# An attention-then-FFN kernel on one core: the order of its steps, its PSUM banks and the choice of masked half rows written anew

## The chip, the cores and the metric

One core of a Trainium2 chip runs the whole program. The metric is device time in microseconds (us), the median of the executions shown. The engines are named as in the profile: PE (TensorE, matmuls; PEld are its weight loads), DVE (VectorE), ACT (ScalarE), POOL (GpSimd) and SP (SyncE, which issues most DMAs). They run side by side, each in its own program order, and wait for each other by semaphores.

## What is computed

Eight batches of eight heads, 576 positions, head size 64; the attention keeps only scores close to the row's maximum; its result, 4608 tokens of 512 values, goes through a feed-forward layer that takes the largest of three products.

```python
scores = scale * np.matmul(q, k.transpose(0, 1, 3, 2))
thresh = np.max(scores, axis=-1, keepdims=True) - tau
scores = np.where(scores >= thresh, scores, -1000000000.0)
scores = scores - np.max(scores, axis=-1, keepdims=True)
attn = np.exp(scores)
attn = attn / (np.sum(attn, axis=-1, keepdims=True) + 1e-09)
x = np.matmul(attn, v)        # then heads side by side: (4608, 512)
h = np.maximum(np.maximum(x @ w1, x @ w2), x @ w3)
out = h @ w_out
```

## The kernel before

The work is cut into small steps, and the order in which the program issues them is written out by hand, as a string of letters (`ORDER`, lines 40 to 74). A loop at the end of the kernel (lines 789 to 796) takes one letter after the other and issues its step. Since every engine takes its instructions in program order, the string sets the order on each engine; between engines only data and buffers matter. A capital letter is a step of PE that opens a PSUM tile, and the digit behind it is the place of that tile: PSUM is used as four slots of two banks (`bank`, line 182).

Four heads of one batch make a quad, 16 quads in all. A quad has nine chunks of 128 rows by two halves (two heads side by side), and each chunk has two half rows r = 0 and 1, 288 in all. Through a half row go, in this order:

- S: scores, float32, on PE, one PSUM slot (`scores`, line 324).
- m: DVE copies the scores to an SBUF tile z, with the sign turned, and takes the row maximum (`maximum`, line 364). There are 9 z tiles, and from the 73rd half row on two more that lent themselves from the weight staging.
- s: DVE makes a threshold out of the maximum (`threshold`, line 375), for code 0 only.
- e: ACT's first pass (`exponents`, line 379); n: ACT's second pass, an exponential with its sum; k: in its place, for masked half rows, a pass of DVE that compares, multiplies and sums (`numerators`, line 388).
- r, once for a chunk: DVE takes reciprocals of the sums. p, once for a half row: POOL scales z into the bfloat16 tile P (`normalized`, line 400; 6 tiles P).
- t, once for a chunk: SP issues a DMA that transposes P into `ptq` (`turned`, line 409).

`MASKED` (lines 24 to 29) gives each half row a code. 0: first pass of ACT from z with the threshold of s, then n. 1: masked, so ACT's first pass is the exponential, from z, and k takes the second pass to DVE. 2: like 0, but ACT reads the scores from PSUM, no s is needed, and the PSUM slot is held until ACT has read it. 3: like 1, but from PSUM.

```python
    def masked(g, idx, r):
        return by_mask[2 * number[g, idx] + r] in "13"
    def direct(c, r):
        return by_mask[2 * number[c["g"], c["idx"]] + r] in "23"
```

The other letters: l loads of q, k and v, g loads of weights, o and i stores of the output (all on SP, with t); z casts of weights, y casts of v and q swaps of the halves of q (POOL, two swaps on DVE); T transposes of q and k on PE (line 293), with a (ACT) and c (DVE) for their copies out of PSUM; O the product of attention and v (line 415), with x (ACT) and w (DVE) for its copies into x of the batch; F and B the two halves of a piece of the FFN (lines 457 and 479), N a last ninth of the output product; h (ACT), v (DVE), u and j (ACT), f (DVE) empty their PSUM. A batch has 18 hidden-layer pieces and its output pieces; they can begin when the four O of the batch are done. Batch 7 is split into two parts, so that its FFN begins earlier.

Of the kernel before, what the change touches and what calls it, by code (L numbers as in the profile page):

```python
# [45 lines left out]
nyrrsmyBepT1svS0hpcT2nS3zmaS1erpgsF2mntpsBmnS3yvF1etssT0myeBprS2cnpS3mnS0ympelF2epF3lmBnzslssvS0htBrqmeS2vpn  # L46
S1gF0sepmF3teqBmF2erssvpBtnBkphF0eS1vtS3znmF2nrBmqteS1rpvBnS3pmlnF0pmgeS1qsBsrhmS3pevS2npS1mF0npsO3ermpesmO2
zewepgsskBxtT3nF1vS2nklBarS0mlphS3mtepF2sS1rmnyBmetF3pvT0eBpcnS2tzT1nvS0asmzS3temS2qeS1meF0trkpmS3lenpBmnlys
reklpF1umerpskS3upBeoketmS0uS2umpS3tesmS1qeT0myO2nqlrsnlprcO3etqsmepwS0xptS1mnF3psnmS2BlerskpS1thF0meF3pmeBF
2ktnBveBsrS1nvpS0hmyF3emF2npBrssT0eprtvBaF1kS3nqvBeF0myhyS2kyleF3mBelBvnpS2snsS0vptemS1pnF3rmpT2tnBmpeF0scS1  # L50
# [5 lines left out]
eBptsF2mhpS1eS3pmteS0qmBeO1spmnkteF3rvnpT0BsskapS2xvS0erS1qmtnS3pmnF2mqlespmeS1rtkBepresmT3puS1cuS0ptmnS3pS2
meyS1lrekpF0tnsmempO3lekteskO2nrsmpeBkpxrnwS1uptS3muS2pnmF0yoeS1mF3lesymBtnS2srkpS1hmBeF0spveF2ertBmpT3nrsvS
1paBlmpnS0tS3qhmF1epsmS2leBymF3tevF0nBknlS1rsvpS2esmqnBF3srmhpS1epS0tmeF2pssBrempBtesvS0ynF1mT3lnpBvF0lhsrcS
2tnT1mBnF3valS2nrBsqmeF0pvS1epS2meBptsmS3eqF1hmT2peBcS3tnskT2O0arkplnmO2lerpvewptS3xkpS1nF2meF0sstreBsmpS3nv
# [1 line left out]
ymeF3pwxskteS0keS1BrrnkopmF2pmS0BqeuurtsmF1phS3srnpS2meT0ptBmeS3ykpaN2esvempF0tS1jkpF3ermBeS2ptvnS1pmBnS0rls
hsmpS2elF3mqntS1mpF0nsrBskpeF2lsmBetBpveF1yhvS3lnkS2lesF0mytnBmBerqsS3veF2lpvnF1pBsmT0htBceF3rT2vnpBsaS0pvnF
1qmtS2nBsrnmT0pS3hrcpF2esS1mpteS0rmpS3emBpntF1svqnS0ssBmpeoT2vO3lamtneF1wS0nrlBpmeS3qsrS2hsmS0pnmF1eptS3smeB
pmF2ntS0veS3rsmnpS1BnpO0veytrempS2empS3xsmS1tekF0nsknlT2rmpBelmlpnscS3quS1umyS2eorT0kpeO3tmeyO1ewlepsmF3etka
rknS2qklT0nBmxespcS2eryF0mpF1uskpuBtnS2BhmqF3nsvS0peS2srmtpF1eBmpeF0srvnBptS2hyS3pmeF1lmeBlBevtF3nkT2S0arrvp
BnS2mphS1smpF0ntS3smnpBmeF1lsT2esvlF3nrBrcptBnvpS2eS0qmlhS1tsnprsmT3F2epmS0aptBemF3yevS1oS0nqmBnpsrS2mnF1ptv
S0epmBeS3mthS2skeF0F1snmlBeklO3ersvpnrmByepF0swT2eqtBvnqF3ssrcS1hpiBmpT0S2vaptS1snmS0pnT3mqF2tecT1BarmS3pnS1
vqeS0mF2pesrmnptmS3npT1seS0qctBeymqermpS1eS3mpuF0nmtuskS1eS2klnS3smBesrsepO1upmemO2txrkpukeO3wnkpS0xS2emF3et
rmS1pnBssspmF2hS0rtepS3mnBpmF1etS0veF3mnN2rnpBpjF0evtF2esBkBkhF1nsvS3eBmBevO3hrkS2pwnS1mnF3prmS2eptsF0mnBpsS
1sevyS2terBmpeF3svS1iyepBmoS0yhmtF2ekF3nBsmS1ersBvpnF0pmeF2BvteS1hBmF3rsS0vpeF1rknpBBmnO2vhptO0xrpnS3pwS2trm  # L70
# [759 lines left out]
```

## Time and profile before

| | us |
|---|---|
| median of three runs | 446.92 |
| lowest and highest | 445.95, 449.74 |
| span of the profiled execution | 444.8 |

The profiled execution's time is listed only among the three runs and not by name; its span, from the first to the last instruction, is 1.1 us below the lowest of them. Other groups of the profile that matter for reading the code:

| group | count | busy us |
|---|---|---|
| scores on PE (two groups, qs and qt) | 1280 | 182.6 and 182.4 |
| hidden-layer products on PE | 2160 | 170.8 |
| ACT first pass from z, with threshold (z tiles) | 143 | 106.2 |
| ACT second pass with sum (z tiles) | 174 | 117.6 |
| DVE maximum (z tiles) | 250 | 183.7 |
| DVE masked second pass (z tiles) | 76 | 62.2 |
| POOL scaling into P (z tiles) | 250 | 200.6 |

Busy times of groups overlap on one engine and don't add up to its busy time. In the rows of the profile, `z` and `stage` are tiles of half rows, `sc` the scores in PSUM, `ph` hidden-layer products, `po` output products, `o` the product with v, `tp` transposes. All instructions of the kernel carry line L93, that of a helper that keeps the order, so groups are told apart by tile.

### The profile page before, as it was taken

The page shows a single profiled execution, that of the slowest core. Times are in us where ns is not written, and L with a number is a line of the kernel's source. Part 1 is how long each engine was busy: PE and PEld are TensorE (multiplying, and loading weights), DVE is VectorE, ACT ScalarE, POOL GpSimd, SP SyncE. Part 2 cuts the span into 40 slices and gives each one's busy share as a digit, 9 for nine tenths or more (in the row PEclk, how much of TensorE's full clock was granted, in tenths as well). Part 3 has the DMA queues.
Part 4 walks back from the last instruction along what each step waited for, and adds up shares of the span by engine and source line. Part 5 has one row for each costly group of instructions (what it writes and reads, how often), then busy time and mean ns, then how long its engine had stood idle before and what let it go on. Part 6 is the DMA issues. An engine that isn't in the chain of part 4 may idle for free.

```text
span 444.8 us, 14254 instructions
## 1 busy us (share of the span) xinstructions
PE 422.4 (95%) x5188; PEld 320.2 (72%) x5190; DVE 392.8 (88%) x1228; ACT 403.0 (91%) x836; POOL 311.9 (70%) x420
## 2 busy tenths in 40 slices
PE   7767789999999999999999999999999999999996
PEld 6334347787788767787788777788688886787873
DVE  3887999999999999999999999998999998899642
ACT  3999999999999999999999999899999999987632
POOL 2799989997878687696785877676676685457400
PEclk8998999999999999999999999999999999999999
DMA  7999999999999999699899999989999977487633
GB/s 188 275 293 199 291 169 269 235 243 262 229 180 194 212 222 292 125 256 167 143 234 189 230 198 203 209 168 210 208 206 194 244 151 105 83 179 136 145 116 108
DMA packets 213959, 88.50 MB, mean 199 GB/s; under 512 B 189184, under 2 KB 202240, under 8 KB 213888
## 3 DMA queue, kind: packets, MB, share of 16 engines
q1 hardware_dynamic: 213360, 86.96, 95.9%
q8 instruction: 41, 0.67, 0.6%
q10 hardware_dynamic: 528, 0.62, 0.5%
q14 instruction: 30, 0.25, 0.2%
HBM read 35.65 MB, written 9.44 MB: 101 GB/s over the span
## 4 chain that ended last, share of the span: by engine, by line
PE 86%; ACT 5%; DVE 4%; issue 2%; DMA 1%; SPq 0%; DVEq 0%; ACTq 0%
PE ph L93 32%; PE sc L93 32%; PE po L93 10%; PE o L93 9%; ACT z L93 5%; PE tp L93 3%; DVE z L93 3%; DMA qm<-in_q_dram 1%; ACT qt L93 1%; SPq L93 0%; DVE xt L93 0%; DVE hm L93 0%; DVE stage L93 0%; DVE rs L93 0%; ACT ob L93 0%
## 5 line engine op out<-in xcount | busy, mean ns | idle before, releaser
L93 POOL TENSOR_SCALAR P<-z,rs 128x576 bf16<-128x576 f32 x250 | 200.6, 814 | 63.3 <-DVE rs L93 28.1
L93 DVE TENSOR_SCALAR_CACHE_REDUCE z<-sc 128x576 f32<-128x576 f32 x250 | 183.7, 750 | 14.8 <-PE sc L93 10.1
L93 PE MATMUL sc<-kt,qs 64*128 64x256 f32 (+2 forms) x640 | 182.6, 423 | 5.7 <-DVE z L93 2.3
L93 PE MATMUL sc<-kt,qt 64*128 64x320 f32 (+2 forms) x640 | 182.4, 433 | 5.2 <-ACT z L93 3.3
L93 PE MATMUL ph<-xt,w 64*128 64x288 bf16 (+2 forms) x2160 | 170.8, 283 | 0.1
L93 PEld LDWEIGHTS <-w 64*128 64x128 bf16 (+1 forms) x2160 | 130.1, 94 | 28.6 <-issue 4.3
L93 ACT ACTIVATE z<-z 128x576 f32<-128x576 f32 x174 | 117.6, 679 | 0.1
L93 PEld LDWEIGHTS sc<-kt,qs 64*128 64x128 f32 (+1 forms) x640 | 92.4, 180 | 25.7 <-DVE z L93 5.7
L93 ACT ACTIVATE z<-z,th 128x576 f32<-128x576 f32 x143 | 106.2, 769 | 5.0 <-DVE th L93 4.2
L93 PEld LDWEIGHTS sc<-kt,qt 64*128 64x128 f32 (+1 forms) x640 | 91.9, 179 | 19.7 <-ACT z L93 5.9
L93 DVE SCALAR_TENSOR_TENSOR z<-z 128x576 f32<-128x576 f32 x76 | 62.2, 830 | 0.5 <-ACT z L93 0.5
L93 PE MATMUL po<-wo,hT 64*128 64x512 bf16 (+3 forms) x454 | 53.5, 354 | 0.3
L93 POOL COPY qs<-qt 64x640 f32<-64x640 f32 (+3 forms) x66 | 43.0, 652 | 10.8 <-ACT qt L93 7.2
L93 ACT ACTIVATE z<-z,nm 128x576 f32<-128x576 f32 x68 | 50.6, 767 | 0.0
L93 DVE TENSOR_TENSOR hm<-ph,hm 128x576 bf16<-128x576 f32 (+2 forms) x54 | 37.0, 686 | 9.2 <-PE ph L93 8.9
L93 ACT ACTIVATE hm<-ph 128x576 bf16<-128x576 f32 (+2 forms) x54 | 31.8, 589 | 13.4 <-PE ph L93 12.8
L93 POOL TENSOR_SCALAR P<-stage,rs 128x576 bf16<-128x576 f32 x38 | 30.4, 804 | 19.3 <-ACT z L93 5.4
L93 PEld LDWEIGHTS <-hT 64*128 64x128 bf16 (+2 forms) x456 | 30.0, 95 | 16.5 <-issue 2.3
L93 DVE TENSOR_TENSOR hT<-ph,hm 128x576 bf16<-128x576 f32 (+2 forms) x54 | 37.0, 686 | 4.0 <-PE ph L93 2.3
L93 PE MATMUL o<-ptq,vb 128*64 128x64 bf16 (+2 forms) x544 | 39.0, 281 | 0.0
L93 ACT ACTIVATION_READ_ACCUMULATOR z<-z 128x1 f32 x174 | 34.3, 197 | 0.0
L93 PEld LDWEIGHTS <-vb 128*64 128x64 bf16 x544 | 23.3, 111 | 12.8 <-issue 4.9
(45 smaller groups left out, 431.6 us busy)
## 6 DMA issues: line engine op xcount, KB each, us to landing
vm<-in_v_dram SPq DMA_DIRECT2D x32, 256.0 KB, 4.8
qm<-in_q_dram SPq DMA_DIRECT2D x15, 512.0 KB, 5.0
km<-in_k_dram SPq DMA_DIRECT2D x15, 512.0 KB, 5.3
out_dram<-ob SPq DMA_DIRECT2D x14, 512.0 KB, 4.0
stage<-in_moe_w_dram SPq DMA_DIRECT2D x9, 512.0 KB, 5.2
ptq<-P SPq DMA_TRANSPOSE x144, 4.0
vr<-in_v_dram SPq DMA_DIRECT2D x16, 128.0 KB, 3.4
stage<-in_moe_w_out_dram SPq DMA_DIRECT2D x3, 512.0 KB, 4.9
```

The lines of the kernel that those rows point to most:

```text
L93: ins = fn(*a, **kw)
```

## The change

Only the two strings are changed: `MASKED` (109 of its 288 codes) and `ORDER` (3465 letters before, 3477 after; the slots' digits not counted). No function is touched. Letters of each kind are the same in number, but for n (202 to 198), k (86 to 90) and s (169 to 181). The codes go from 169, 78, 33 and 8 of kinds 0, 1, 2 and 3 to 181, 86, 17 and 4. Below are all codes; of the order its first five lines (the start, up to the first F), then the lines with the 10th to 12th O and with the 19th and 20th O, and its end. All the other lines change in the same way.

```diff
 MASKED = """
-232222322322222222021032222202332122123122200200111000000000100000000011
-000010111020011000101000000001100001001000010011111100000000100100000000
-110010030111000100010000000001010100001110001011010100110000000000000000
-100101101011000000120000001010000000110000011100000001110001000010011111021
+112200200001110011002221222020211232320300202100110000000000100000100011
+000011101001000100110000000000110000011000011010101000100001000010001000
+110010010011100101000000001000110100000001101101001100010100001000001000
+100001010110110000000000000010100000011010111011001010000010100010103021
 ORDER = """
-llllllglllT0laclT1laclzllqqS0qqS1meS2mS3lmlT0enlkS1ylmlT2eamelrnpS3leqlmnyS1qcapS0emtnrcS3pmnT2qmepgrelS1qya
-gS0pmelT2mqnS3tcpemqS2nlkT1eytaS0rmnT1kpermS3yS2enczrmS1qT0enmepnqtS3nprmaymgpeS0lptS2mppT0mtpS1enencnqsS3re
-rmtpS0mS1penmS3lqnsS2mtperpekzllmT0tmpenkT1pgS3eearnS0petmnqrS2meqlnpS3lmnplsS2cetpremS1pS0nmplermtzeS3mnS2p
-mtnpmS3rkpS1leektS0emnrpmemptS1eekS2pO3mktS0rennmpermT2pnS1wptemS3prkyO0tmeakS2pgS1enxlnrmS0lpesS2mezT3mS1np
-mgntspcS2eqrseT3mtpeS0srmapS1mnT2ptS3mnqO0ceqmeO1prswnptnkS3pxS0meF1meS2zBresmT0qghF3klpF2nkBtaS1sveS0pemF3B
+llllllgllT2lcaqqlT3S0alcqqmS1lzS3elmS2gmS0elmelkeT1lkaT2nlqS3maqlnsmS0qgeqrrscS3ylecmnS2lpmS1nlpmepsserS2mzS
+0lesmS1pnmS2ynlpmS3nprmT1eS0ymgpaT2lspsnT3mT1ezcS0esrqS2akeptcelmpT1eknqmerqkS3etqalrekpS2gnmnS0psmteysS3emp
+nrS1kpT2emntT0yrmepncytS3pnrS2mpetmpaS1repS3mtepknpS2ntmS0elzmelmS1pnlsS3rmpnT2rspectmepS2epgS0mnqmS2eqS0tme
+qS1emlqO3nrklpnweptrnmS2zeO3mepknpS1xrS0metpmnT2pS3rketpasS1meS0ptrmeT2psnkS1tpemnzrmtS0nscS3pemtepS2knT0qS1
+atmnrlS0rspmempeS2tmyngO1meplssrepS2lwnS3gpmeS0lkqO2elmelmyT1xpS3srceS0pmF2npS1mnBqtmnF3qsrhkT0pBakS1esS2veF
...
-O1ypersmqO2etkpemO0lewqxlknpS3tS1keF2momS3lexF0ktT1enkBercpnsBpumN1ertkphkF3jS0rursS1empBnmF2ptS0vpS1smeF3yt
+mS2nS0mtS3ermpO1esspmnO2yemnkyO0tesrkpewF3epkxS2reBymxpkelqF2ulS0npBlmnN1srshkptuT0nS2cqF3jmyS0erS1semBptnmF
...
-pBnmS1tS2hmT3eF0rmpnF1cBpnBrevptT3S2apvS0qmtS3S1enmqF2esrsqmiepmleS0soykeS1plBnmemtS3ukS0uT1snrlO2cpekynO1me
+rmpesmepO0knuO1wekuT3ekF0xrrclpeS2slpnBmpktpF2ursS3uS1pemBopmS0nlyS3hmF1emS2teS0srsmpT3nBmeN2vatkeqS1lkjF0on
...
-2tvF3vF1hF2voF3vF1ohF2vF3vF1hF2vO3vO1wF2xuuF1oF0hiF3vF1vF0hF3vF1vF0hF3vF1vF0hF3vF1vF0hF3vF1vF0huF3vF1ovF3uoF
-0uoN1fjdi
+F3voF2hF1vF3vF0htF2vF3vF0hF2vF1vF0hF2vF3vF1hF2vO3vO2wF0xF2uF1hF0voF3vF1hiF0vF2vF1hF3vF0vF2hF1vF0vF3hF2vF0vF1
+hF3vF2vF0uF1ouN3ofjdi
 """
```

More of the change, by code (lines that the diff above doesn't have):

```diff
@@ L24 @@
 MASKED = """
-232222322322222222021032222202332122123122200200111000000000100000000011
-000010111020011000101000000001100001001000010011111100000000100100000000
-110010030111000100010000000001010100001110001011010100110000000000000000
-100101101011000000120000001010000000110011100000001110001000010011111021
+112200200001110011002221222020211232320300202100110000000000100000100011
+000011101001000100110000000000110000011000011010101000100001000010001000
+110010010011100101000000001000110100000001101101001100010100001000001000
+100001010110110000000000000010100000011010111011001010000010100010103021
 """
@@ L46 @@
[L46 to L50, printed above, removed]
@@ L51 @@
-htBrnmpF3erT2rpvlBasS1pstvnS2pmeF0pS3emtBqnmT2S1hcqS3empF2eS0rsqmtS1epsmBeF3pmnF0stsvBeBknF2klhF1BvelS0nrvpB
-emT3pS2arvS0ptnS3mpnO1smtesrkpeF2swnlrpmeT0S1qtescS3epBmnpmnT0trskS3paS1umS0ulqmeS3lmyS1nopS2smelS0rmeS3psmn
-O1ypersmqO2etkpemO0lewqxlknpS3tS1keF2momS3lexF0ktT1enkBercpnsBpumN1ertkphkF3jS0rursS1empBnmF2ptS0vpS1smeF3yt
-BsnsmBpnvS0pT1hmF2atT3srepS0cF1eprBsmeqF3vnByBynvplS2nsS0plmhS1mteS2mF0nF3mteS1rrspBnmS2pelvBlepF1smT0leqBvl
-aS2rkhF3oqnsS0mtS1epmBeqsF2ssmtS0epvBeyF1mnF3vpBesrS0ktphBermS1npT2svO0nytmpncT3eS1wF2nrmS0aBrsmnqF3vnT1pS0c
@@ L56 @@
[L56 to L59, printed above, removed]
-pBnmS1tS2hmT3eF0rmpnF1cBpnBrevptT3S2apvS0qmtS3S1enmqF2esrsqmiepmleS0soykeS1plBnmemtS3ukS0uT1snrlO2cpekynO1me
@@ L61 @@
[L61 to L70, printed above, removed]
@@ L71 @@
-npS0mnF3pmteF1pBeBvtS0rS2vpS3empF1ktkF0kBereskpemBkperumO2uptO3xpN1wtenkO2jrF3pxF1hpF2nvF3tvF1rhF2pvF3pvF1hF
-2tvF3vF1hF2voF3vF1ohF2vF3vF1hF2vO3vO1wF2xuuF1oF0hiF3vF1vF0hF3vF1vF0hF3vF1vF0hF3vF1vF0hF3vF1vF0huF3vF1ovF3uoF
-0uoN1fjdi
+llllllgllT2lcaqqlT3S0alcqqmS1lzS3elmS2gmS0elmelkeT1lkaT2nlqS3maqlnsmS0qgeqrrscS3ylecmnS2lpmS1nlpmepsserS2mzS
+0lesmS1pnmS2ynlpmS3nprmT1eS0ymgpaT2lspsnT3mT1ezcS0esrqS2akeptcelmpT1eknqmerqkS3etqalrekpS2gnmnS0psmteysS3emp
+nrS1kpT2emntT0yrmepncytS3pnrS2mpetmpaS1repS3mtepknpS2ntmS0elzmelmS1pnlsS3rmpnT2rspectmepS2epgS0mnqmS2eqS0tme
@@ new lines @@
+qS1emlqO3nrklpnweptrnmS2zeO3mepknpS1xrS0metpmnT2pS3rketpasS1meS0ptrmeT2psnkS1tpemnzrmtS0nscS3pemtepS2knT0qS1
+atmnrlS0rspmempeS2tmyngO1meplssrepS2lwnS3gpmeS0lkqO2elmelmyT1xpS3srceS0pmF2npS1mnBqtmnF3qsrhkT0pBakS1esS2veF
+0psrmF3tnpsBmeBzrvtT1hS2spceF0ptmnS3zS1semT2tnBmpS3avqF1ntsrsT0mynBgpscS2elprS3empS0nmtyF2nmF3eyBvpS0erpS1mh
+BztemF2nF0syvBqtnsBvgpeS3rlkhS1pgF2emF0lnssqmBlnBpvlS3esrvS1peF2mpeF0sBsmnqS3hrBpmnS1tpvnS3zsmeS2F0rempS1epO
+3metknO2gmerwpnBtskxpT3lF1evS2lakBnqS0mhS3rmtpF2esS1srpesmT0epBmF3npvtT1eBzcS2avzntS0mS1eymF2etmnqkS0etyS3sr
@@ new lines @@
+lmeBpsnkpeF1meyrkpS0usuS3mtpnBmleqlrkS0puS2umT3etpS1smeS0qrscO2npmeyssO3ewtpnrmoS1pxlS2empS0lnskF3lnF1mBermB
+pthF2speS0vyeBrmpF1nvS3ypnF0mnBtkBhF2ketF1ssveBlS3revplT0emBlaS2klS3hqmlF0nrF1rpsmnBpnBvtF3peslvS2qnrS0smpeS
+1moeyT2BmlF0phslcS1npF3meBpsT2vBaS1srnvpS2temF0plS3esmBnrmpT2thS1cynS3qmlS0epsF2meS1qmeF3rtkBpeF0lvnBlpmnBF2
+khF1nsrtrBpveS0spveT3BmpaS2ssvnS0tqS3mepO1metqmeT0yweS3tsncF2emtnS1rkpS3nrmtT0nBprsmapsekS1puS0mutS3epsmS1ep
+mS2nS0mtS3ermpO1esspmnO2yemnkyO0tesrkpewF3epkxS2reBymxpkelqF2ulS0npBlmnN1srshkptuT0nS2cqF3jmyS0erS1semBptnmF
@@ new lines @@
+2plS0evplS1nmF3eBrmptBnsvpT1hS0skeF2smaT3BrncptF1esS0rpvF3erpmtBepS2lvnS0lpmBeymS1ynpS2stmhF0eomF3nlS1skeS2o
+rmpBnBsvqnF1mT0ptBvaS2hsrS0pemF3pemS1S2nrqsmBtemF0pnF1vqtBekBpS2ssvhtF3nqmT0BercptS2snrsvlpO0elmpelT3pswF2nk
+S1aS0rmetqBmeF3pT1veS0pceBF2mhS1nktS0esmlS3BemO1nmtnkF0ynvT3xBtrsrspS2aveS1ymiqS3emS0pnsF2rpemynmpT3S1tecpS0
+rsnmBpempteS1sklpS3emF0urkptumnS1lS2qemoO3qemnpskO2telrekpBlxsknwS1uprS2umtS3pemF0epS1smnBsmF2hoS3esrkS1peBm
+F0ntyvF3elBrmpeT2svBpatS1rkhpS0lnmF2S3npmS1tesrqmF0BnmpF3esrvpBteBslvqS1hlspS2nmF3pnrmS0tepS1smBepsF2mtnpS0v
@@ new lines @@
+eBmeF3trT1vnpBcnF0yS2khBemT1F3nrsvS2alsBemqF0rvS1nptS2empS3esmpBF1mhpT2ekBytS3nclqT0esklO2pamesO0rtvekeF1ywx
+S3snBymyF0ntprS2svnlpS3rmlBpS1mhpS2emT3tqF0esscqF1nsBmtpnT3rvBlpaS2evqS0emS3pemS1tpeF2srmpnmqeS0kS3tpnS1mlnB
+rmpesmepO0knuO1wekuT3ekF0xrrclpeS2slpnBmpktpF2ursS3uS1pemBopmS0nlyS3hmF1emS2teS0srsmpT3nBmeN2vatkeqS1lkjF0on
+sF3mlBerpS2vepBmS1phrS0tnmpF3emS2pS1ntsmBerF0smpeF2tskpBeBvtF1hrvpS3nskpS2temF0nBrmptBnsF3vpeS2vtnBmF1hT0rep
+BceT2qF3sveS0lskaBnF1mqS2tnpvBermT0pS3hcpF2nlsmS1elS0rsmpS3nsmBqetF1rmpS0nvpBemO3evntsT2weF1sS0skatS3emqBnmS
@@ new lines @@
+2phS0rmpF3esS1mpeBsrmytnF2pvS0npBemtS1eklS3sO0rveptmnpS2mxyS1nrsmpT3nF0smytescepS2S1eymyBnmlekS3lurS1kpuO2re
+mteqmO0nwpeskpT1xF3kalreT1pS0ecS2pnlmBpnrmiyS0uoF2umpF1ersBkqBhsF3eqvtS0epS2mnS1pmBnpF0stveF2smBeF3tskhBnBvt
+nS1rvpT2eF0smpatS3erBslqrmS2hpS1nmS3tpnmF0opeT2smBpnF1vF3etscBeBrsvpS2npS0hmtnS1mT3eF2srsmpaS0teBqmlS1npvF3e
+S0mqnBrmqnS2spstvF1eS0pmeS3smeBS2mhF0emtF1ekBnO3srvpnkpeT0sBweF2rsvpF3nBpercS1tphBsmnT0pvS2atS1mnqT3S0semqtF
+2ecT1BramS3nqsvS1npS0mnF2pmermpeT1S3cpeS0trsmBpnmeqS1sketyS3nmpF0urmyepkS1upS3etmBeorsmpeS1kpuS3muO2nkkoO0xy
@@ L74 @@
+merO2ewptkpS3xssS0nmF1terF2mpBrkpS3thsS0emBpemF1pS3evN0temekF2tjkBnrF3spvnS0pBnmF1yhrkBpeF0vBtnyrsBpvO2hpisr
+eS1wpS0mnptF2esS3mpeS1tsmBeF0vnF3tmBnS2resvpS1emBpS0nmF2nrmF1phBsktpeBvS0erF3svpnF2mpBetS1shS0mnBekF3tF1emBn
+rvBpsO0hvpO2xrkpeS1wS0nmptF3meS2rF1spmeBptBevS0nvS2S3mF1tsmekF0nmerBkpnreBpukpuO2urO1pxtuO2pwoN0pxF3jF2thF0v
+F3voF2hF1vF3vF0htF2vF3vF0hF2vF1vF0hF2vF3vF1hF2vO3vO2wF0xF2uF1hF0voF3vF1hiF0vF2vF1hF3vF0vF2hF1vF0vF3hF2vF0vF1
+hF3vF2vF0uF1ouN3ofjdi
 """
```

## The prediction

> **What bounds the kernel now.** I read the page's first two parts, then the windows of the start, the middle and the end, then the chain, then the waits, and last single rows of the timeline for prices.
>
> ```profile
> span 444.8 us, 14254 instructions
> PE 422.4 (95%) x5188; PEld 320.2 (72%) x5190; DVE 392.8 (88%) x1228; ACT 403.0 (91%) x836; POOL 311.9 (70%) x420
> PE   7767789999999999999999999999999999999996
> ACT  3999999999999999999999999899999999987632
> 9.00:73.00 64.00, 50.07 (x442) 28.66 (x441) 56.34 (x170) 61.59 (x134) 56.30 (x75) 0.93 1.12 247
> 80.00:430.00 350.00, 348.68 (x4515) 273.98 (x4513) 323.03 (x1019) 328.33 (x679) 248.19 (x331) 1.00 0.98 195
> 430.00:445.00 15.00, 10.44 (x72) 6.31 (x71) 4.62 (x9) 3.71 (x8) 0.00 (x0) 0.98 0.23 80
> PE 86%; ACT 5%; DVE 4%; issue 2%; DMA 1%; SPq 0%; DVEq 0%; ACTq 0%
> ```
>
> The three rows of windows (length, then busy PE, weight loads, DVE, ACT, POOL, clock, DMA) split the run into stages with different limits. From 80 to 430 us PE is busy 348.68 of 350 us: 1.3 us of idle time is all that a better order of this stage could win by closing gaps. In the last 15 us PE misses 4.6 us; the last 22 F and the last N of both orders follow each other with nothing else for PE between them, so that stays. In the first 73 us PE is idle 64 - 50.07 = 13.9 us of a 64 us window, and there ACT is the full engine, 61.59 of 64 us. So the kernel has an ACT-bound start, until the first hidden-layer product can run, and from there PE sets the pace. A change wins or loses in two ways: the moment at which the FFN products start, and new gaps in PE's middle.
>
> ```profile
> 72.37 0.64 ACT L93 ACTIVATE xt<-o 128x576 bf16<-128x576 f32 x1
> 73.06 0.67 PE L93 MATMUL ph<-xt,w 64*128 64x288 bf16 x8
> ```
>
> The first hidden-layer product starts at 73.06 us, straight after ACT's copy of the last quarter of x of batch 0 (72.37 + 0.64 = 73.01). That copy is the second letter x of the order, so what ACT has to do ahead of the second x decides the start.
>
> **The start, counted.** Prices are distances from start to start, since instructions overlap on ACT and DVE:
>
> ```profile
> 35.80 0.72 ACT L93 ACTIVATE z<-sc,nm 128x576 f32<-128x576 f32 x1
> 36.42 0.67 ACT L93 ACTIVATE z<-z 128x576 f32<-128x576 f32 x1
> ...
> 111.59 0.76 ACT L93 ACTIVATE z<-z,th 128x576 f32<-128x576 f32 x1
> 112.26 0.76 ACT L93 ACTIVATE z<-z,nm 128x576 f32<-128x576 f32 x1
> 112.92 0.67 ACT L93 ACTIVATE z<-z 128x576 f32<-128x576 f32 x1
> 113.50 0.19 ACT L93 ACTIVATION_READ_ACCUMULATOR z<-z 128x1 f32 x1
> 113.59 0.67 ACT L93 ACTIVATE z<-z 128x576 f32<-128x576 f32 x1
> ```
>
> A first pass over a half row (letter e) costs 0.67 us from SBUF and 0.62 us straight from PSUM (36.42 - 35.80); a second pass with its sum (letter n) costs 0.67 us (113.59 - 112.92). Ahead of the second x the old order has 49 e, 37 n and 10 a; the new one 50 e, 32 n and 10 a, because more of the first half rows are masked (codes 1 and 3 do their second pass on DVE, letter k). Of those e the old masks read 37 from PSUM (codes 2 and 3), the new ones 19. So ACT saves 5 x 0.67 = 3.35 us, pays one e, 0.67, and pays 18 x 0.05 = 0.9 us for reading from SBUF: 1.8 us less.
>
> What DVE pays for it, with PE's work up to there:
>
> ```profile
> 114.25 0.74 DVE L93 SCALAR_TENSOR_TENSOR z<-z 128x576 f32<-128x576 f32 x1
> 114.91 0.08 DVE L93 DVE_READ_ACCUMULATOR z<-z 128x1 f32 x1
> 114.91 0.75 DVE L93 TENSOR_SCALAR_CACHE_REDUCE z<-sc 128x576 f32<-128x576 f32 x1
> 115.59 0.08 DVE L93 DVE_READ_ACCUMULATOR z<-sc 128x1 f32 x1
> ...
> 119.49 0.15 DVE L93 TENSOR_SCALAR th<-nm 128x1 f32<-128x1 f32 x1
> 119.55 0.75 DVE L93 TENSOR_SCALAR_CACHE_REDUCE z<-sc 128x576 f32<-128x576 f32 x1
> ```
>
> A masked second pass takes 0.66 us and a threshold 0.06 us. Ahead of the second x: k 12 to 14, s 8 to 18, so 2 x 0.66 + 10 x 0.06 = 1.9 us more, less one kt copy that comes later. DVE was busy 56.34 of 64 us there, so its 7.7 us of idle time cover it; without that cover the 1.8 us would be gone. PE's letters up to the first F are the same, 54 S, 16 T and 4 O: nothing is postponed. So the first F starts about 1.8 us earlier, **-1.8 us**, and PE carries this through the middle. Over the whole run DVE gets 4 more k and 12 more s, 4 x 0.66 + 12 x 0.06 = 3.4 us, against 27 us of idle time in the middle window (350 - 323.03); ACT loses 4 n (-2.7) and pays 20 x 0.05 = 1.0.
>
> **Slots and z buffers** cost nothing by count: between the letter that frees a bank and the S that takes it again lie at least 5 steps of the order in the middle (3 before), half of them 9 or more (8 before). Half rows that hold a z tile when a new one is made are 8 or fewer in most cases (9 before). Both go the way of fewer waits, and there is little left to win in the middle.
>
> **Transposes (letter t) and loads on SP's queue.** This is the large move. The letter t stood a median of 7 steps behind its second p and now stands 29 behind; SP works in order, so whatever stands ahead of a t holds it.
>
> ```profile
> L93 PE MATMUL o<-ptq,vb x544: 190/272/404, 55.2 to 424.4; 128*64 128x64 bf16 x86, 128*64 128x512 bf16 x75, 128*64 128x256 bf16 x21
> L93 SPq DMA_TRANSPOSE ptq<-P x144: 1241/1432/4678, 17.6 to 418.9; - x144
> who waited for it (us, times):
>   DVE xt L93: 2.3, 5
>   ACT xt L93: 2.2, 2
>   PEld L93: 0.2, 1
> DMA to landing us min/median/max: 3.2/4.0/8.1
> SPq L93 <- POOL P L93: 130.9, 83, 6.0
> SPq L93 <- PE sc L93: 5.8, 8, 2.4
> L93 POOL TENSOR_SCALAR P<-z,rs x250: 734/746/1857, 14.7 to 418.1; 128x576 bf16<-128x576 f32 x125
> ```
>
> Today SP stands in front of a t and waits for P, 83 times and 130.9 us; a t is issued as soon as P is there and lands after 4.0 us, and PE waited for no transpose (its weight loads 0.2 us once). The products run from step 309 (55.2 us) to step 2834 (424.4 us) of the old order, which is 369.2 / 2525 = 0.146 us per step. The shortest way from a chunk's last p to the product that reads it was 27 steps at the very end and 31 in the middle; it becomes 30 (the 19th O), 32 and 36, and the others are longer. By need it is 0.75 us of P and 4.0 us of transpose, 4.75 us; 30 steps are 4.4 us. If SP issues each t when P is there, one product waits 0.4 us and the rest nothing: that is the lower bound. If a t is issued only where it is written, the distances t to O decide: 13, 16, 20 and 22 steps are 1.9, 2.3, 2.9 and 3.2 us against 4.0 us, a shortfall of 2.1 + 1.7 + 1.1 + 0.8 = 5.7 us: the upper bound. I take **+0.3 us**, near the lower end, since SP waits for P in most cases and an earlier issue is then free.
>
> Of 28 q and k loads, 10 now stand 5 to 17 steps behind the transposes (letter T) that free their tile, where all but the first stood 41 or more behind. SP may hold there; the longest hold for PE's scores was 2.4 us. Behind such a load stand the next t and vm loads; their readers are 20 or more steps off, so I cost it at nothing, and at 2.4 us where it meets one of the tight products.
>
> **The sum.** 444.8 - 1.8 + 0.3 = 443.3 us of span. The lowest of the runs, 445.95, lies 1.1 us above the profiled span, the median, 446.92, 2.1 above it; the difference taken off the median gives 446.9 - 1.5 = **445.4 us**.
>
> **Rivals.**
>
> ```profile
> ACT z L93 <- DVE z L93: 2.4, 3, 1.3
> PEld sc L93 <- ACT z L93: 10.0, 19, 1.0
> ...
> 252.38 1.17 PE sc L93 x6
> 256.05 0.93 PE sc L93 x6
> ...
> 74.99 1.53 PE ph L93 x24
> 126.33 2.94 PE ph L93 x48
> ```
>
> *The start gains more.* The first two rows are waits of the first 70 us. ACT's idle time there, 2.4 us, waited for maxima of DVE, and scores waited 10.0 us for banks that ACT held by reading from PSUM. With 18 fewer such reads this could vanish: 446.9 - 1.8 - 2.4 = 442.7 us. Against it: DVE gets 1.9 us more work in the same stage.
>
> *PE's middle is not full.* A pair of scores took PE 0.93 us in one place of the chain and 1.17 us in another. If the new neighbours moved one pair in ten from the long to the short form, that is 14 x 0.24 = 3.4 us: 446.9 - 1.8 - 3.4 = 441.7 us. Against it: the hidden-layer products go at 1.53 us for 24 and 2.94 us for 48, 61 to 64 ns each wherever they run, which is one pace and not a stalled one. The Trainium skill (Trainium Kernel Development and Optimization, Performance Expectations) says that matmul busy time is a poor measure of the distance to the limit, and that the share of weight loads is a better one. By that rule the 72% of the page would leave PE room in the middle, and the order could win there. No run here shows by how much.
>
> *Transposes come late (slower).* SP comes to the t late because loads ahead of it hold, and the four tight products wait on PE: 5.7 us by the written places, and one hold of 2.4 us: 446.9 - 1.8 + 8.1 = 453.2 us. It decides from the point where a product's first weight load waits more than 1 us for ptq.
>
> *The start's gain is not carried.* By the 73rd F the new order has 3 fewer n, 1 more e and 20 fewer reads from PSUM, which is -2.0 + 0.7 + 1.0 = -0.3 us for ACT. If ACT and not PE is the limit up to there, only 0.3 us are left: 446.6 us. Against it ACT has idle time in the middle, 350 - 328.33 = 21.7 us.
>
> **Chances.** The forecast 0.42 (its own range 443.5 to 447), more at the start 0.20, a fuller middle 0.08, late transposes 0.20, gain not carried 0.10. A measurement of this kernel tells about 1%, 4.5 us, from no change: faster is below 442.4, slower above 451.4. A little under half of the second case, most of the third and a tail of the first are faster: 0.19. Two thirds of the late transposes are slower, with what else may go wrong: 0.15. The same: 0.66. The range goes from 441 (both gains) to 452 (the late transposes without a hold, 450.8, and a little more).
>
> **What would show it.** The first ph at about 71.3 us and ACT as full as now before it; PE idle time of 80 to 430 us still below 2 us; no PE wait for ptq above 1 us. Wrong if ph starts no earlier, if PE's middle has gaps of several us, or if weight loads of o wait for transposes.

## The result and the profile after

| | before | after |
|---|---|---|
| median (12 runs each) | 447.49 us | 450.75 us |
| lowest, highest | 445.95, 449.74 | 447.74, 452.77 |
| profiled span | 444.8 us | 448.8 us |

The changed kernel takes 1.0065 times as long as the kernel before, with a 95% interval of 1.0038 to 1.0092: about 3 us slower, where 1.5 us faster had been forecast. The range held the time; the direction was wrong. The medians and ratios here leave out an execution that was over 1.5% above the fastest of its kernel, one each in experiments 8 and 14.

The page of the changed kernel, its span, its busy times and the slices of PE and ACT:

```profile
span 448.8 us, 14304 instructions
PE 422.2 (94%) x5190; PEld 315.6 (70%) x5190; DVE 397.7 (89%) x1248; ACT 402.5 (90%) x828; POOL 317.3 (71%) x420
PE   6767788999999999999999999999999999999996
ACT  4899798999999999999999998999999998998522
```

PE is as long busy as before (422.2 against 422.4 us), in a span that is 4.0 us longer. So PE was idle 26.6 us where it was idle 22.4. ACT's row shows a 7 at the fifth slice (45 to 56 us) and an 8 at the seventh, where before it was full.

The windows of the same kernel (length, then busy PE, weight loads, DVE, ACT, POOL, clock, DMA):

```profile
9.00:73.00 64.00, 47.34 (x422) 27.19 (x418) 55.06 (x178) 58.39 (x123) 54.97 (x71) 0.92 1.13 242
...
80.00:430.00 350.00, 348.15 (x4534) 268.85 (x4531) 327.39 (x1030) 331.18 (x681) 254.51 (x334) 1.00 0.98 195
430.00:449.00 19.00, 14.74 (x104) 9.31 (x102) 6.59 (x13) 4.70 (x10) 0.00 (x0) 0.98 0.21 70
```

From 9 to 73 us PE does 47.34 us of work instead of 50.07, and from 80 to 430 us it is idle 1.85 us instead of 1.32. In the 7 us between, where it had been full, it is idle 1.7 us. The time shows as work left over for the end: 14.74 us behind 430 us, where 10.44 were left. ACT, which was the full engine of the start (61.59 of 64 us), has fallen to 58.39. So something else than ACT holds the start now, and the next rows say what. They are the first product of P with v, on GpSimd, on SP's queue and on PE (start, length, engine, operation, and in brackets the idle time before it and what ended it):

```profile
38.84 1.47 POOL L93 TENSOR_SCALAR P<-z,rs 128x576 bf16<-128x576 f32 x2 [0.80 <-DMA ptq<-P]
...
43.50 1.32 SPq L93 DMA_DIRECT2D vr<-in_v_dram  x2
44.92 0.57 SPq L93 DMA_DIRECT2D qm<-in_q_dram  x1
45.58 1.34 SPq L93 DMA_TRANSPOSE ptq<-P  x1
...
49.38 0.40 PE L93 MATMUL o<-ptq,vb 128*64 128x512 bf16 x1
51.73 1.68 PE L93 MATMUL o<-ptq,vb 128*64 128x512 bf16 x14 [1.95 <-DMA ptq<-P]
```

The P of the first quad's ninth and last chunk is ready at 40.3 us (38.84 + 1.47). Its transpose stands behind two earlier transposes, two loads of `vr` and a 512 KB load of `qm`, and SP comes to it at 45.58 us, 5.3 us after P. The product needs it at 49.8 us and gets it at 51.7. The issues of 44 to 53 us in the two kernels (median time from issue to landing), the changed one first:

```profile
ptq<-P SPq DMA_TRANSPOSE x3, 6.1
```

```profile
ptq<-P SPq DMA_TRANSPOSE x4, 5.1
```

A transpose took 6.1 us there, and 5.1 us in the kernel before. (The ninth one took 6.2 us in the kernel before too, but its product came at 55.2 us and did not notice.) The forecast had counted with 4.0, the median of the whole run. The Trainium skill (DMA: Bandwidth & Descriptors, Queues, rings and completion order) says that a DMA engine consumes the descriptors of a queue in the order of its ring; a transpose issued just behind 512 KB then starts behind them, and the 6.1 us agree. Experiments 1 to 3 repeat this landing and its opposite.

The second gap of the start, again on SP's queue and on PE:

```profile
68.53 0.39 SPq L93 DMA_DIRECT2D stage<-in_moe_w_dram  x1
...
70.08 0.52 SPq L93 DMA_DIRECT2D stage<-in_moe_w_dram  x1
70.65 0.63 SPq L93 DMA_DIRECT2D qm<-in_q_dram  x1
...
74.31 0.69 PE L93 MATMUL ph<-xt,w 64*128 64x288 bf16 x8
...
78.14 0.46 PE L93 MATMUL tp<-identf,qm 64*128 64x64 f32 x8 [1.66 <-DVE th L93]
```

The issues of 66 to 80 us have the landing of that load:

```profile
qm<-in_q_dram SPq DMA_DIRECT2D x1, 512.0 KB, 7.4
```

From 68.53 us on SP issues loads without a transpose between them, two of them 512 KB of weights ahead of the queries `qm` of the fifth quad. The transposing product that reads `qm` starts at 78.14. The load landed at 70.65 + 7.4 = 78.05. The row names a threshold `th` of DVE, which ended at 78.06, but PE reads no thresholds; in experiments 1 and 5 the row names the load, and with small loads the wait is gone (experiment 10). The first hidden-layer product starts at 74.31 us: 1.25 us later than before, not 1.8 earlier. The third place is in the middle, again in the timeline:

```profile
170.98 1.15 PE L93 MATMUL o<-ptq,vb 128*64 128x512 bf16 x14 [0.62 <-DMA ptq<-P]
```

All transposes of the run, issue to landing:

```profile
DMA to landing us min/median/max: 3.2/4.5/8.8
```

It is the 11th product, the one whose last transpose is written 13 steps ahead of it. That transpose landed 3.2 us after its issue, as fast as any in this run; it was issued late, at 167.70 us. The median landing rose from 4.0 to 4.5 us.

### The profile page after: what moved, and what is told of

Read it like the earlier page. It is cut to its first block, busy times and chain, and to the rows that moved or that the text cites. A ratio compares the mean times of both kernels' runs of the same rounds, so it can differ in the third digit from the quotient of the medians.

```text
span 448.8 us, 14304 instructions
## 1 busy us (share of the span) xinstructions
PE 422.2 (94%) x5190; PEld 315.6 (70%) x5190; DVE 397.7 (89%) x1248; ACT 402.5 (90%) x828; POOL 317.3 (71%) x420
## 4 chain that ended last, share of the span: by engine, by line
PE 69%; POOL 8%; DVE 6%; issue 6%; ACT 5%; DMA 4%; SPq 1%; POOLq 0%; DVEq 0%; ACTq 0%
PE ph L93 29%; PE sc L93 22%; PE po L93 8%; PE o L93 7%; DVE z L93 5%; POOL P L93 4%; ACT z L93 4%; DMA ptq<-P 3%; PE tp L93 3%; POOL qs L93 2%; DMA qm<-in_q_dram 1%; SPq L93 1%; POOL vb L93 1%; POOL w L93 0%; DVE stage L93 0%
## 5 line engine op out<-in xcount | busy, mean ns | idle before, releaser
L93 PE MATMUL sc<-kt,qs 64*128 64x256 f32 (+2 forms) x640 | 177.6, 415 | 5.4 <-POOL qs L93 1.8
L93 PE MATMUL sc<-kt,qt 64*128 64x320 f32 (+2 forms) x640 | 178.5, 426 | 4.4 <-DVE z L93 2.6
L93 PE MATMUL ph<-xt,w 64*128 64x288 bf16 (+2 forms) x2160 | 168.4, 283 | 0.0
L93 PEld LDWEIGHTS <-w 64*128 64x128 bf16 (+1 forms) x2160 | 127.9, 94 | 27.9 <-issue 4.3
L93 ACT ACTIVATE z<-z,th 128x576 f32<-128x576 f32 x156 | 116.1, 768 | 3.5 <-DVE th L93 3.2
L93 DVE SCALAR_TENSOR_TENSOR z<-z 128x576 f32<-128x576 f32 x77 | 64.0, 837 | 0.8 <-ACT z L93 0.7
L93 POOL COPY qs<-qt 64x640 f32<-64x640 f32 (+3 forms) x66 | 46.7, 707 | 24.1 <-ACT qt L93 21.0
L93 ACT ACTIVATE z<-z,nm 128x576 f32<-128x576 f32 x73 | 55.3, 769 | 1.3 <-DVE z L93 1.3
L93 DVE TENSOR_TENSOR hm<-ph,hm 128x576 bf16<-128x576 f32 (+2 forms) x54 | 37.0, 685 | 11.4 <-PE ph L93 10.9
L93 PE MATMUL o<-ptq,vb 128*64 128x512 bf16 (+2 forms) x544 | 40.8, 285 | 3.3 <-DMA ptq<-P 2.6
L93 PEld LDWEIGHTS <-hT 64*128 64x128 bf16 (+2 forms) x456 | 27.7, 95 | 18.6 <-issue 2.0
```

The lines of the kernel that those rows point to most:

```text
L93: ins = fn(*a, **kw)
```

## The experiments

Theory A: the change loses its time where a transpose or a load arrives late over DMA. Theory B: the new masks and thresholds load DVE and ACT in another way, and the DMAs are innocent. Each ratio below is against the kernel before, measured beside it on the same chip.

| kernel | median us | ratio | 95% interval |
|---|---|---|---|
| changed kernel | 450.75 | 1.0065 | 1.0038 to 1.0092 |
| 1 ninth transpose early | 449.44 | 1.0052 | 1.0032 to 1.0072 |
| 2 loads of the fifth quad early | 452.00 | 1.0094 | 1.0066 to 1.0123 |
| 3 both | 452.05 | 1.0110 | 1.0083 to 1.0137 |
| 4 new masks, old order | 476.09 | 1.0652 | 1.0622 to 1.0681 |
| 5 all transposes at their p | 457.23 | 1.0230 | 1.0200 to 1.0260 |
| 6 the same from the fifth quad on | 453.43 | 1.0144 | 1.0123 to 1.0165 |
| 7 as 5, with 2 | 455.29 | 1.0183 | 1.0157 to 1.0209 |
| 8 old order, transposes late | 465.33 | 1.0379 | 1.0336 to 1.0423 |
| 9 kernel before, small loads | 447.09 | 0.9998 | 0.9980 to 1.0016 |
| 10 changed kernel, small loads | 445.24 | 0.9967 | 0.9947 to 0.9988 |
| 11 as 5, small loads | 449.70 | 1.0038 | 1.0010 to 1.0066 |
| 12 small loads in the start only | 447.14 | 1.0006 | 0.9979 to 1.0033 |
| 13 small loads behind it only | 447.60 | 1.0012 | 0.9994 to 1.0029 |
| 14 v loads from GpSimd | 460.31 | 1.0290 | 1.0253 to 1.0327 |

**1. The ninth transpose early.** A number behind l, t or p counts the letters of its kind from 0; behind S, T and O it is the slot.

```diff
-... l26 ... l27 ... l28 ... T2 r s p e c t8 m e p
+... t8 ... l26 ... l27 ... l28 ... T2 r s p e c m e p
```

> The changed order with one letter moved: the transpose of the first quad's last chunk (t number 8, from 0) stands ahead of the three loads of v and q that now stand before it on SP's queue. Theory A (the time is lost where a DMA arrives late in the start): t8 is issued at about 43.5 us instead of 45.6, lands by 47.5, the first product at 49.4 us no longer waits, and ACT and DVE lose no 2.7 and 3.3 us behind it: 2 to 3.5 us faster than the changed kernel, about 447.5 to 448.5. Theory B (the masks and the thresholds load DVE, so the start is slower whatever the DMAs do): PE then waits for DVE instead, less than 1 us faster.

The wait at 52 us is gone, but that alone proves little. Experiments 2 and 6 keep the changed order up to this product, and in their profiles it does not wait either, so a wait of 2 us there is not in every execution. What recurs is the landing. The ninth transpose from issue to landing, behind the loads (experiment 2) and ahead of them (experiment 3):

```profile
ptq<-P SPq DMA_TRANSPOSE x1, 5.7
```

```profile
ptq<-P SPq DMA_TRANSPOSE x1, 3.3
```

Behind the loads it took 5.7 to 6.1 us in the changed kernel and in experiments 2 and 6, ahead of them 3.3 us in experiments 1 and 3. The timeline of experiment 1 shows waits at the next readers:

```profile
67.86 1.12 PE L93 MATMUL o<-ptq,vb 128*64 128x512 bf16 x14 [1.70 <-DMA ptq<-P]
77.80 0.46 PE L93 MATMUL tp<-identf,qm 64*128 64x64 f32 x8 [1.99 <-DMA qm<-in_q_dram]
```

By the ratios the kernel is 0.6 us faster than the changed one, where 2 to 3.5 us were expected, and that is within the noise. The start ran into the second quad's product, whose transpose stands 20 steps ahead, and then into the same `qm`.

**2 and 3. The loads of the fifth quad early, alone and with 1.**

```diff
-... l31 S0 ... l32 ... l33 ... l34 ... l35
+... l31 l32 l33 l34 l35 S0 ...
```

> The changed order with four loads moved: q and k of quad 4 (l 32 to 35) stand directly behind l 31, ahead of t18 and of two weight loads. Theory A: q of quad 4 lands before 76.5 us instead of 78.05, PE's wait of 1.7 us ahead of the transposes at 78 us goes, 1 to 2 us faster than the changed kernel; the wait of the first product stays. Theory B: nothing changes by more than 0.5 us.

> Both moves together. Theory A: 3.5 to 5 us faster than the changed kernel, about 446 to 447, level with the kernel before or up to 1.5 us below it, since the first 47 us of the changed order were 1.7 us ahead. Theory B: still above 449.

Both missed on the far side. Experiment 2 removed the wait at 78 us, and products waited for transposes elsewhere, 1.40 us at 278 us and once in the start, as its timeline shows (the profiled execution took 456.3 us, 4.3 us above this kernel's median):

```profile
67.39 2.05 PE L93 MATMUL o<-ptq,vb 128*64 128x512 bf16 x14 [1.48 <-DMA ptq<-P]
```

Neither of the two stands behind the moved loads: the transpose of the row above is issued ahead of them, at 64.00 us, and lands 3.2 us later, and at 278 us the order is the changed kernel's. What the moved loads do delay is the transpose behind them, issued at 68.74 us instead of 66.77 and landed 8.7 us later; no product waited for it. Experiment 3 was level with the kernel before at 82 us (its first hidden-layer product came at 73.23) and lost in the middle; PE's largest gap there was 1.71 us, at the same 11th product. What SP does earlier for one reader, it does later for another; which of these delays made the two kernels slow is not shown.

**4. The new masks on the old order.** The order of the kernel before, with the letters s, n and k changed only where the new codes ask for them.

> The order of before with the new masks alone: each half row that becomes masked has its n turned into k at the same place, the other way round likewise, and a half row that needs a threshold gets its s right behind its m. Theory A (the masks are not the cause): ACT's saving of about 1.8 us in the start shows or is lost to places that do not fit, between 2 us faster and 1 us slower than the kernel before. Theory B (the masks are the cause): 2 to 4 us slower than the kernel before, with ACT idle for maxima or thresholds of DVE.

This kernel is no clean test. Its scores waited for ACT; from the waits of PE up to 95 us:

```profile
PE sc L93 <- ACT z L93: 13.4, 9, 2.4
```

It was 4.0 us in the kernel before. An order is made for its masks, and neither half can be judged inside the other. The reverse pair, the old masks on the new order, was not tried on the chip.

**5, 6 and 7. The transposes back at their p.**

```diff
-p(2c+1) ... (some 30 letters) ... t(c)
+p(2c+1) (7 letters) t(c)
```

> The changed kernel with every transpose (letter t) put back to some 7 steps behind the second p of its chunk; nothing else moves. The way from the last t to its product becomes 61, 77 and 36 steps at the first three products (26, 43, 20 in the changed order), 24 and 32 at the 11th and 12th (13, 20), 23 and 27 at the 19th and 20th (16, 20). Theory A (products wait on PE for late transposes): no wait of o for ptq above 1 us at 52, 68 or 171 us, 2 to 4 us faster than the changed kernel, 446.5 to 448.5 us. Rival C (SP now holds for P in front of the loads, so that loads of q, k, qm and km come later): ptq waits vanish, but scores or T wait longer for loads, and the time stays at 449 to 452 us. Rival B (the new masks load DVE, the transposes are innocent): the time stays at 450 to 451 us and DVE's and ACT's idle time of the start stays as it is.

> The transposes are early only from the fifth quad on (chunk 36 and later); the start of the changed kernel is left as it was. Theory A splits: the wait of the 11th product at 171 us and the like go (about 1 us in all, since the middle of the changed kernel lost 0.5 us more than before's), the start's loss of 3.9 us of PE work stays: 449.5 to 450.5 us. If it comes out as low as the first of this set, the loss was in the middle; if the first of this set is lower by 2 us or more, it was in the start.

> As the first of this set (all transposes some 7 steps behind their p) and the loads of q, k, qm and km of the fifth quad put four places up, behind the load of the weights that came just ahead of them. Theory A: with the transposes early the wait of the transposed queries for qm at 78 us goes too (it was 1.7 us), and nothing new waits: 445.5 to 447.5 us. Rival C (SP holds): the early loads delay transposes or the other way round, 449 us or more.

None came out as theory A wanted. Rival C, SP's hold, was right and stronger than expected. The largest of SP's own waits in experiment 5 (us in all, times, longest):

```profile
SPq L93 <- POOL P L93: 155.3, 94, 5.8
```

Its timeline around the place:

```profile
71.90 0.65 PE L93 MATMUL ph<-xt,w 64*128 64x288 bf16 x8
...
74.20 0.59 SPq L93 DMA_DIRECT2D qm<-in_q_dram  x1
...
79.63 0.69 PE L93 MATMUL tp<-identf,qm 64*128 64x64 f32 x8 [5.55 <-DMA qm<-in_q_dram]
```

With the transposes early the first hidden-layer product starts at 71.90 us, 1.2 us ahead of the kernel before. Then SP, which has waited 155 us for P instead of 128, issues `qm` at 74.20 instead of 70.65, and PE stands still for 5.55 us. Experiment 7 put these loads in front; PE's gaps were then at 94 us (1.83 us, for DVE) and at 171 us (3.34 us, for `ptq`). Experiment 6 left the start alone, and the 11th product waited 3.86 us although its transpose was written 24 steps ahead instead of 13. So the late letter t has a use in this order: in the start it lets the loads pass.

**8. The mirror: the old order with late transposes.** The last one to four transposes of a quad moved to some 14 to 17 steps ahead of the product, at eleven places.

```diff
-... p t ... p t ... (26 to 73 letters) ... O
+... p ... p ... t t (14 to 17 letters) O
```

> The kernel before (its order and masks) with the last transposes of a quad written late, so that the first of the two products at eleven places (3rd, 5th, 7th, 11th, 15th, 19th, 23rd, 25th, 27th, 29th, 31st O) stands 14 to 17 steps behind its last t where it stood 26 to 87 behind; nothing else moves. At 0.146 us per step that is 2.0 to 2.5 us against a landing of 4.0 us. Theory A: eight or more of these products wait 1 to 2 us on PE; where PE is full (all but the first) that is lost: 5 to 12 us slower than before, 452 to 459 us. Rival (SP and PE run with enough slack, or PE's sequencer takes later work to fill it): the waits are under 0.5 us each and the time is within 2 us of before.

(The expectation's 87 should read 73.) Only five products waited, not eight, and it cost 17 us by the ratio, more than was expected. The waits of PE and of GpSimd, and the timeline at the largest one:

```profile
PE o L93 <- DMA ptq<-P: 15.5, 5, 7.2
...
POOL P L93 <- DMA ptq<-P: 4.1, 3, 2.4
```

```profile
127.21 0.45 SPq L93 DMA_DIRECT2D qm<-in_q_dram  x1
...
128.49 8.33 SPq L93 DMA_TRANSPOSE ptq<-P  x3
...
137.13 2.05 PE L93 MATMUL o<-ptq,vb 128*64 128x512 bf16 x14 [7.18 <-DMA ptq<-P]
```

The second row of the waits was not expected. The kernel has six buffers for P, and a transpose that is not issued holds one; four held transposes leave GpSimd two. GpSimd stood still for transposes, and SP, with its queue in order, then waited 5 us of the 8.33 for GpSimd. So this run shows that late transposes alone make PE wait, without any other edit, but not their price in the changed kernel: there GpSimd waited 1.4 us for transposes in all.

**9, 10 and 11. Small loads.** The loads of q and k of the third quad and later fetch an eighth, those of v a quarter; the rest of the tile keeps older values. The tiles of a quad are those of the quad two before, so that nothing unwritten is read.

```diff
-L[n] = ld.tile([128, 16, D], F32, name=n + "m")
+L[n] = Ls[g - 2][n] if g >= 2 else ld.tile([128, 16, D], F32, name=n + "m")
...
+if g >= 2 and i is None:
+    return t[:, :, 0:1], rows_of(src)[:, 2 * qd:2 * qd + 2, 0:1]
...
+n = 256 if g < 2 else 64
```

> The kernel before, with the loads of q, k (512 KB) and v (256 KB) of the third quad and all later ones cut to an eighth and a quarter: they fetch one column block of eight for q and k, one fourth of v, and the rest of the tile keeps the values of the quad two before. Order, instructions and issues stay. Base for the next two. PE's waits for qm were 2.2 us in all and for ptq none, so theory A (only late arrivals cost) expects 443 to 447 us; theory D (the DMA engines, busy all the time to 350 us, set the pace themselves) expects 440 us or less.

> The changed kernel with the same small loads. Theory A (the change loses time where loads and transposes arrive late): waits for qm and ptq (3.3 and 2.6 us) fall below 1 us together, the first hidden-layer product comes at 71 to 73 us, and the kernel is 0 to 2 us faster than the same cut of the kernel before, where it was 3 us slower. Theory B (the new masks and their DVE work, or the order of scores): it stays 2 to 4 us slower than the same cut of the kernel before.

> The changed kernel with every transpose 7 steps behind its p, with the same small loads. Full loads made this one 6.5 us slower than the changed kernel by a wait of 5.6 us for qm. Theory A, size of loads: the wait for qm falls below 1.5 us and it is within 2 us of the changed kernel with small loads. Theory A, time of issue: SP stands in front of the transposes and issues the loads late, small or not; the wait for qm stays above 2.5 us and it stays 3 to 7 us slower than the changed kernel with small loads.

This pair decides between A and B. On the kernel before, small loads bring nothing (0.9998). On the changed kernel they bring 4.4 us by the ratios, and now it is the faster of the two: 445.24 against 447.09 us. B, which wanted it 2 to 4 us slower still, falls, and so does D for the kernel before, which the DMA engines alone do not pace. The page of experiment 10 and its window of the middle, then the page of experiment 9:

```profile
span 444.9 us, 14302 instructions
PE 421.2 (95%) x5188; PEld 316.0 (71%) x5190; DVE 399.0 (90%) x1248; ACT 402.3 (90%) x828; POOL 317.6 (71%) x420
```

```profile
80.00:430.00 350.00, 348.75 (x4515) 269.29 (x4514) 326.63 (x1023) 329.77 (x679) 252.46 (x332) 1.00 0.84 151
```

```profile
span 445.9 us, 14254 instructions
PE 423.9 (95%) x5188; PEld 322.1 (72%) x5190; DVE 393.7 (88%) x1228; ACT 403.1 (90%) x836; POOL 312.0 (70%) x420
```

No product waits for `ptq` any more in experiment 10, and nothing waits for the fifth quad's `qm`. (PE's waits for `qm` stay at 3.2 us in all, not below 1 as expected; they lie ahead of 15 us, where the loads are full.) All transposes land sooner, too: the median fell from 4.5 to 3.7 us, and from 4.0 to 3.5 us on the old order. The row of experiment 10:

```profile
DMA to landing us min/median/max: 3.2/3.7/6.4
```

Experiment 11 splits the two ways in which a load delays. Its timeline at the fifth quad's `qm`:

```profile
73.84 0.58 SPq L93 DMA_DIRECT2D qm<-in_q_dram  x1
...
77.57 0.46 PE L93 MATMUL tp<-identf,qm 64*128 64x64 f32 x8 [2.25 <-DMA qm<-in_q_dram]
```

The load is issued as late as in experiment 5 (73.84 and 74.20 us): that is SP's hold, and small loads do not shorten it. The wait fell from 5.55 to 2.25 us. Of this 1.7 us was size (this load landed 5.3 us after its issue in experiment 5 and 3.6 here); the rest is an issue 0.4 us earlier and a PE that came 1.2 us later. The edit does not change bytes alone: the loads also write other tiles and so wait for other readers, and in experiment 10 this `qm` is issued at 67.92 us instead of 70.65. So "small" stands for both, landing sooner and being issued at another time; the new tiles with full loads throughout were not tried. Early transposes cost 4.5 us with small loads (449.70 - 445.24) and 6.5 with full ones (457.23 - 450.75); by the ratios it is 3.2 and 7.4.

**12 and 13. Where the small loads count.** The same edit for the third to the fifth quad alone, and for the sixth and later ones alone.

> The changed kernel, with the loads of q, k and v small for the third to the fifth quad only (the ones that the start waits for); all later loads are full. With all loads small it was 5 us faster than the changed kernel, in the profiles 2.7 us of it by the 60th maximum and 1.2 us after it. Theory A, start: 446.5 to 448.5 us, the 60th maximum at 82 to 83 us, no wait for ptq before 80 us. Theory A, middle: 449 to 450.5 us, hardly better than the changed kernel.

> The mirror of the one before: loads full up to the fifth quad and small from the sixth on. Theory A, start: the start stays as in the changed kernel (60th maximum at 84 to 85 us), the wait of the 11th product at 171 us goes, 448.5 to 450 us. Theory A, middle: 446 to 447.5 us.

Either half brings over half of it. By the ratios, the changed kernel is 2.9 us above the kernel before; with small loads in the start 0.3 us of it is left, with small loads behind it 0.5 us, and with both it is 1.5 us below. One alone brings about 2.5 us, both together 4.4, each uncertain by about 1 us. So late arrivals seem to cost in both parts, but experiment 13 is no clean test of the second. Its loads of the start are full, and yet its start did not stay as it was: the 60th maximum (letter m) came at 82.7 us instead of 84.7, the first hidden-layer product at 72.50 instead of 74.31. The new tiles are in use there from the third quad on, and single executions differ as well (73.60 in experiment 6, which has the changed start). How much of the loss lies behind the start stays open.

**14. The loads of v from GpSimd's queue.**

```diff
-sync.dma_start(out=L["vm"]...    sync.dma_start(out=L["vr"]...
+pool.dma_start(out=L["vm"]...    pool.dma_start(out=L["vr"]...
```

> The changed kernel with the loads of v issued from GpSimd's queue in place of SP's; bytes, order and all else stay, and the result is the reference's. SP held 23 us in front of v loads for GpSimd's casts and then issued transposes in bursts. If SP's holds are what makes transposes late: no wait for ptq at 171 us, the wait at 52 us stays (it stands behind a q load), 448 to 449.5 us. If GpSimd pays more for the issues than it has idle (it is 71% busy, 86% in the start): P comes later and it is slower, 452 us or more. If the DMA engines' time is all that counts: 450 to 451.5 us.

The busy times of its page:

```profile
PE 428.4 (93%) x5188; PEld 319.5 (70%) x5190; DVE 400.5 (87%) x1248; ACT 403.6 (88%) x828; POOL 348.0 (76%) x468
```

The 48 issues cost GpSimd 348.0 - 317.3 = 30.7 us, 0.64 us each, and P came later: SP waited 166.9 us for P, where it was 128.1. Products waited 1.6 us for `ptq` instead of 2.6, which says nothing certain about SP's holds, since everything else moved as well.

No kernel that computes the whole output was faster than the kernel before.

## Why the prediction was wrong

**The start, -1.8 us: the count was fair, the condition failed.** The step said that the first hidden-layer product would come 1.8 us earlier because ACT had that much less to do, and that nothing else was postponed. The trace has it 1.25 us later; in experiment 6, which has the same start, it is 0.5 us later. Where the arrivals are in time, the gain is there in part: 71.90 us in experiment 5, 71.66 in experiment 12 and 73.18 in experiment 10, against 73.06 before and 73.78 in experiment 9. By 10 against 9 that is 0.6 us, by 12 against 9 it is 2.1; single profiles of the same order differ by almost 1 us there, as the 73.06 and 73.78 or the 74.31 and 73.60 show, so the size of this gain is not settled. What failed is "ACT as full as now": PE waited 1.95 us at the first product and 1.66 us at the fifth quad's queries, and ACT, which lives on PE's scores, ran dry.

**Transposes, +0.3 us: the wrong end of the bounds, and one product missing.** This step failed, and the next with it: together they were to cost 0.3 us, and the late arrivals cost 4.4 (experiment 10 against the changed kernel, by the ratios). The lower bound rested on SP being in front of a t before P is there. SP still waited for P 128 us in all, almost as before, but not at the tight products: there it came to the t late, behind loads or in a row of other transposes, at the first product 5.3 us after P was there. The list of tight products had four with 13 to 22 steps; the first one, with 26 steps or 3.8 us, was left off it against a landing of 4.0. There the landing was 6.1. The upper bound of 5.7 us was near what the late arrivals cost in all (4.4 us, or 450.75 - 445.24 = 5.5 us by the medians), though not at the four products that made it up. The rival "transposes come late" named this mechanism with its sign and its condition (a wait above 1 us for `ptq`), and it is what happened in the profiled execution, at 52 us, with a smaller wait of 0.62 us at 171 us; its price, 453.2 us, was 2.5 us too high. The six buffers for P, which a late transpose holds, were not counted either. (The prediction's 29 steps from a second p to its t are 31.5 in the median by a count of the new order; its sum does not use them.)

**Loads close behind their T: costed at nothing.** They were the other half of the mistake, though not by the holds that the prediction had in mind. SP waited 10.9 us, up to 4.7 at a time, for the T that free the tiles, where it was 0.4 us before and the prediction had allowed 2.4; but 7.7 us of this lie between 260 and 350 us, where PE waited for no transfer, and in the fast experiment 10 it is 19.4 us. What cost time is what stands behind or beside a load. Experiments 2 and 5 show that loads and transposes share SP's time, and the landing times of experiments 1 to 3 and 9 to 11 that they share the DMA engines. In the windows of the middle the DMA engines have a share of 0.98 in the changed kernel and of 0.84 with small loads. The prediction had read SP's queue as a line of waits and had left out that the engines behind it were full, though its own rows of windows show a DMA share of 1.12 and 0.98.

**Slots, z buffers and DVE's extra work: no cost seen.** DVE got 4.9 us more work (397.7 against 392.8) and stayed off the path; experiment 10 has even more of it and is the fast one.

**PE's middle: the rival with a chance of 0.08 was in part true.** Scores became cheaper. All instructions that touch scores, from 100 to 400 us, in the kernel before, the changed kernel and experiment 10 (busy PE is the first number):

```profile
100.00:400.00 300.00, 132.68 (x916) 75.87 (x916) 153.41 (x416) 2.19 (x3) 1.00 1.00 196
```

```profile
100.00:400.00 300.00, 130.82 (x924) 78.51 (x924) 154.15 (x418) 0.00 (x0) 1.00 1.02 201
```

```profile
100.00:400.00 300.00, 130.04 (x920) 77.80 (x918) 154.11 (x419) 0.00 (x0) 1.00 0.86 152
```

That is 145 ns for a score before and 141 to 142 ns after; over 1280 scores some 4 us. Experiments 9 and 10 agree: PE is busy 2.7 us less, while its idle time is 1.7 us more, 23.7 against 22.0. So the 1.5 us that the order gains with small loads are not the 1.5 us of the forecast: ACT's saving was forecast, and cheaper scores are what the profiles show. Which neighbours make a score cheaper was not tried.

**The sum as it turned out.** PE's idle time went up by 4.2 us. Its busy time stayed, and in it cheaper scores met dearer work of other kinds. The products of P with v kept PE busy for 44.13 us before, 46.22 now and 44.36 in experiment 10. Of the 2.1 us more, 1.3 lie ahead of 60 us (4.17 us there, 2.85 in experiment 10), and the last section says why. The other 2 us or so are not accounted for.

## What to carry to other kernels

In an order where one queue issues everything, a transfer's place costs twice: by what it waits for and by what it stands behind. Before a transfer is moved, list its slack in microseconds against the landing time of its own neighbourhood (here 6.1 us behind a 512 KB load, not the median of 4.0), and list also what is then let past or held. When DMA engines are busy for most of the span, fetch less in one run as a test: it costs one kernel, and it tells an order's own worth from what its transfers take back. And before one wait in one profile is called the cause, look whether it is there in the profile of another kernel with the same order up to that point: the wait of 2 us at the first product was not.
